# Sliding-window attention with a highway layer: gates of the first tiles a step later, other orders of loads, completions and the sinks' work, and a fused last tile

## The chip, the cores and the metric

The kernel runs on one core of a Trainium2 chip. The metric is the device time of one execution in microseconds; three runs of the kernel before have a median of 116.3 us (115.77 to 116.56). A profile of one further execution gives what every engine did and when; times inside it are counted from the start of its span.

## The reference

Attention over 4 batches, 8 heads, 768 positions and 64 values a head, in which a query sees the 4 first positions (the sinks) and the 128 positions up to its own. Its output, with the heads side by side, is the input x (3072 x 512) of a highway layer.

```python
scores = scale * np.matmul(q, k.transpose(0, 1, 3, 2))
keep = is_sink | in_window              # pos < 4, or 0 <= q_pos - k_pos < 128
scores = np.where(keep, scores, -1000000000.0)
a = softmax(scores)
x = (a @ v), heads side by side         # (3072, 512)
H = np.maximum(x @ w_h, 0.0)
T = 1.0 / (1.0 + np.exp(-(x @ w_t + b_t)))
out = T * H + (1.0 - T) * x
```

## The kernel before, in words

The 3072 rows are 24 tiles of 128 (N = 24, six to a batch, NC = 6). A loop of 26 steps, written out by hand (L471 to L544), is a pipeline: step n computes the scores of tile n, the attention output of tile n - 1 (`n1`), the gate and hidden products of tile n - 2 (`nb`), and completes an earlier tile. Every engine takes its instructions in the order in which the program has them; `_keep_traced_order` (L24) fixes that. So does each DMA queue: SP's, POOL's and, at the start, ACT's.

What a tile goes through, with the engine and the line:

- `scores` (L265, TensorE): a mask by matmul (L272) and q times k (L279) into `ps_s`, of which there is one; `expo` (L323, ACT) reads it into `E`.
- `starts` (L305, TensorE): the bias of the gate into `ps_z` (L311) and the sinks' part of the values into `ps_av` (L317).
- `values` (L330, TensorE, L338 and L341): `E` times `v`, which `cast_v` (L141) has cast from fp32, on VectorE for tiles 0 to 4 and on POOL from tile 5 on (`LATE`).
- `norm` (L346, VectorE): reciprocal of the sum (L349) and the product `X` (L351).
- `x_transpose` (L359, TensorE, L362) and `x_copy` (L365, ACT, L367): `XT`.
- `gate` (L369, TensorE, L371) into `ps_z`, `tanh` (L376, ACT, L378) into `TH`. The logistic function is 0.5 tanh(z / 2) + 0.5; the outer half is `gate_value` (L380), on VectorE, on POOL for the tiles in `POOL_GATES` (L73), and on ACT for the last two.
- `hidden` (L387, TensorE, L390) into `ps_h`, `diff` (L400, VectorE, L403): relu(hidden) - X into `DD`.
- `complete` (L423): `gate_value`, `gated` (L407, VectorE, L408: `DD` times `TH`), `finish` (L411, L414: plus `X`, on POOL, for tile 22 on VectorE) and the store by SP (L416).

The sinks of a batch need keys masked by head (`sink_keys`, L251), values masked by head (`sink_values`, L260, on POOL), the products of all queries with them (`sink_scores`, L286, L293) and an exponential (`sink_expo`, L299, L301). In step 2 of a batch they are made for tiles 2 to 5 (`sinks_at`, L452); for batch 0 it is done in two halves, in steps 2 and 4.

q and k come as fp32 and are cast to fp16 by loads on POOL's queue (`load_part`, L105; `load_rows` takes four of them), except the first two thirds of q of batch 0, which SP and ACT load as fp32. `transpose_qk` (L118, VectorE, L125) puts them where the scores read them; `units` (L429) says in which step which part is transposed, `loads` (L441) in which step which part is loaded. Batches 0 and 1 come in thirds, 2 and 3 in halves. V comes on SP's queue (`load_v`, L129), the two weights on POOL's (L194, L196). `completed` (L448) says which tiles a step completes: tile n - 6 in steps 6 to 12, 7 and 8 in step 13, n - 5 in steps 14 to 20, then two each in steps 21, 22 and 23 and tile 22 in step 24. `idle` (L418) issues matmuls on zeros, 18 before the loop, 5 in step 0, 3 in step 1. Tile 23 is completed behind the loop (L546 to L555).

Of the kernel before, what the change touches and what calls it, by code (L numbers as in the profile page):

```python
# [11 lines left out]
FP32 = mybir.dt.float32  # L12
# [25 lines left out]
def kernel(  # L38
# [33 lines left out]
    LATE = 5  # L72
    POOL_GATES = range(12, 16)  # L73

# [97 lines left out]
    def load_sinks(b, gs=range(G)):  # L172
        for g in gs:
# [5 lines left out]
              allow_small_or_imprecise_dtypes=True)  # L179
    load_rows(0, 0, 1)  # L180
    for g in range(G):
        pool.iota(vmask[32 * g:32 * g + 32, :], pattern=[[-NSINK, H]], base=0,
                  channel_multiplier=1, allow_small_or_imprecise_dtypes=True)
# [7 lines left out]
    pool.dma_start(out=brow[0:P:32, :], in_=moe_b_t.unsqueeze(0).to_broadcast([G, DM]))  # L191
    load_rows(0, 1, 1)
    load_rows(0, 2, 0)
# [46 lines left out]
    def sink_masks():  # L240
        dve.memset(skmask, 0.0)
        for g in range(G):
            for hg in range(HG):
                h = hg * G + g
                dve.memset(skmask[32 * g:32 * g + 32, hg, h:h + 1], 1.0)
# [134 lines left out]
    def gate_value(n):  # L380
        if n >= N - 2:
            act.activation(out=TH[n], in_=TH[n], func=AF.Copy, scale=0.5, bias=0.5)
        else:
            (pool if n in POOL_GATES else dve).tensor_scalar(  # L384
                out=TH[n], in0=TH[n], scalar1=0.5, scalar2=0.5, op0=ALU.mult, op1=ALU.add)
# [37 lines left out]
    def complete(m):  # L423
        gate_value(m)
        gated(m)
        finish(m, eng=dve if m == N - 2 else pool)


    units = {}  # L429
    for b in range(1, B):  # L430
        if b == 1:
            for n, i, which in zip((5, 5, 6, 7, 8, 9), (0, 0, 1, 1, 2, 2), (0, 1) * 3):
                units.setdefault(n, []).append((b, i, which))
        else:
# [11 lines left out]
    for n in range(8, N):  # L446
        v_at[n] = (n + 4,)
    completed = {n: (n - 6,) for n in range(6, 13)}  # L448
    completed[13] = (7, 8)
    completed.update({n: (n - 5,) for n in range(14, 21)})  # L450
    completed.update({21: (16, 17), 22: (18, 19), 23: (20, 21), 24: (22,)})
    sinks_at = {2: (0, (2, 3)), 4: (0, (4, 5))}  # L452
    for b in range(1, B):
        sinks_at[b * NC + 2] = (b, (2, 3, 4, 5))
# [3 lines left out]
    act.copy(out=nat[0][0][:, 0, 1], in_=first[0][:, 1])  # L458
    sink_masks()
    ones_columns()  # L460
# [3 lines left out]
    dve.tensor_copy(out=nat[0][1][:, 0], in_=first[1])  # L464
    transpose_qk(0, 1, 0)
    transpose_qk(0, 1, 1)
    sink_keys(0, dve)
    cast_v(0, dve)

    idle(18)  # L470
    for n in range(N + 2):  # L471

        nb, n1 = n - 2, n - 1
        if n < N:
# [5 lines left out]
            if n % NC == 3 and n // NC + 1 < B:  # L480
                load_sinks(n // NC + 1)
        if 4 <= n <= 6:
            hidden(n - 4 if n < 6 else 3)
        if n == 0:
            idle(5)
        starts(n1 if 0 <= n1 < N else None, nb if nb >= 0 else None)
        if 0 <= n1 < N:
            values(n1)
        if LATE <= n < N:
            cast_v(n, pool)  # L490
# [4 lines left out]
        for b, i, g, which in loads.get(n, ()):  # L495
            load_part(b, i, g, which)

        if 4 <= n <= 6:
            diff(n - 4 if n < 6 else 3)
        if n == 3:  # L500
            transpose_qk(0, 2, 1)
        turn = list(units.get(n, ()))
        if n == 5:
            transpose_qk(*turn.pop(0))
        if 0 <= n1 < N:
            norm(n1)
        if 0 < n < LATE:
            cast_v(n, dve)
# [4 lines left out]

        if nb >= 0:
            gate(nb)
            tanh(nb)
        if n == 5:
# [12 lines left out]
        if 6 <= n <= N:  # L530
            hidden(nb, range(KC // 2, KC))
        done = completed.get(n, ())
        for m in done[:-1]:
# [57 lines left out]
```

## Time and profile before

| | |
|---|---|
| median of three runs | 116.3 us (115.77 to 116.56) |
| the profiled execution | 114.55 us |
| its span | 112.8 us |
| TensorE clock granted, mean | 0.996 |
| TensorE matmul busy | 98.4 us (87%), 1414 instructions |
| VectorE busy | 87.5 us (78%), 184 instructions |
| ScalarE (ACT) busy | 76.6 us (68%), 95 instructions |
| GpSimd (POOL) busy | 87.2 us (77%), 141 instructions |
| moved by DMA | 20.81 MB, mean 185 GB/s |

A row of the timeline has the start, the time from the start of the first to the end of the last of the instructions that it merges, the engine and line, the operation, what is written from what, shapes, the count, and in brackets how long the engine had stood idle before it and what ended that. PE is TensorE, DVE is VectorE. Slices of the span show the busy share in tenths. A matmul's time in a row includes its way through the array, so that a row of TensorE rarely shows a short wait.

### The profile page before, as it was taken

How to read it: one execution, taken by the hardware profiler on the slowest of the kernel's cores; microseconds unless marked ns; L12 is line 12 of the kernel's file. 1: busy time of each engine (PE TensorE's matmuls, PEld its weight loads, DVE VectorE, ACT ScalarE, POOL GpSimd, SP SyncE). 2: the span in 40 equal slices, each digit the busy share in tenths (PEclk: the TensorE clock that was granted, in tenths of full speed). 3: DMA queues.
4: the chain of work that ended last, by engine and by line, in shares of the span. 5: the costliest groups of instructions: out<-in, count | busy, mean ns of one | idle time of the engine just before them, and what ended most of it. 6: DMA issues, size and time to landing. Idle time of an engine off the chain costs nothing.

```text
span 112.8 us, 3577 instructions
## 1 busy us (share of the span) xinstructions
PE 98.4 (87%) x1414; PEld 51.5 (46%) x1414; DVE 87.5 (78%) x184; ACT 76.6 (68%) x95; POOL 87.2 (77%) x141
## 2 busy tenths in 40 slices
PE   5986389899989998999999979999999999977900
PEld 2322246345435454655455535644555566523500
DVE  6796587535677986889998998699777979999660
ACT  4476639985557786788587868687678987842520
POOL 6899997249599499997899999999758965866100
PEclk9999999999999999999999999999999999999998
DMA  3999999999999749989998999899994503324222
GB/s 97 222 234 214 210 201 224 192 204 242 212 241 150 112 139 233 256 193 237 203 207 205 224 239 261 166 209 210 242 259 131 162 6 136 143 99 176 103 111 75
DMA packets 36704, 20.81 MB, mean 185 GB/s; under 512 B 27340, under 2 KB 33232, under 8 KB 36688
## 3 DMA queue, kind: packets, MB, share of 16 engines
q1 hardware_dynamic: 29680, 13.50, 46.6%
q0 software_dynamic: 6848, 6.82, 38.6%
q10 hardware_dynamic: 160, 0.26, 0.8%
q8 instruction: 11, 0.18, 0.7%
q14 instruction: 5, 0.04, 0.1%
HBM read 21.11 MB, written 6.29 MB: 243 GB/s over the span
## 4 chain that ended last, share of the span: by engine, by line
PE 39%; DVE 22%; POOL 14%; DMA 14%; issue 7%; DVEq 1%; POOLq 0%
POOL nat L109 11%; PE ps_h L390 9%; DMA wh<-in_moe_w_h_dram 9%; PE ps_z L371 8%; DVE tr L125 7%; PE ps_s L279 5%; DMA nat<-in_k_dram 5%; DVE DD L403 4%; DVE TH L384 4%; PE ps_av L341 4%; PE ps_av L338 3%; PE ps_s L272 3%; DVE DD L408 2%; PE ps_av L362 2%; DVE X L351 2%
## 5 line engine op out<-in xcount | busy, mean ns | idle before, releaser
L327 ACT ACTIVATE E<-ps_s,ebias 128x2048 f16<-128x2048 f32 (+1 forms) x24 | 43.8, 1825 | 12.6 <-PE ps_s L279 12.6
L414 POOL TENSOR_TENSOR O<-DD,X 128x512 f32<-128x512 f16 x22 | 25.4, 1156 | 10.1 <-DVE DD L408 4.2
L390 PE MATMUL ps_h<-wh,XT 128*128 128x512 f16 (+1 forms) x96 | 27.4, 375 | 0.2 <-DMA wh<-in_moe_w_h_dram 0.2
L125 DVE STREAM_TRANSPOSE tr<-nat 128x384 f32<-128x384 f32 (+1 forms) x28 | 25.7, 957 | 2.3 <-DMA nat<-in_k_dram 1.9
L109 POOL DMA_DIRECT2D nat<-in_k_dram x40 | 21.9, 554 | 5.5 <-DMA wh<-in_moe_w_h_dram 3.7
L371 PE MATMUL ps_z<-wt,XT 128*128 128x512 f16 x96 | 24.6, 379 | 0.0
L403 DVE SCALAR_TENSOR_TENSOR DD<-ps_h,X 128x512 f16<-128x512 f32 (+1 forms) x24 | 16.2, 673 | 8.2 <-PE ps_h L390 8.1
L367 ACT COPY XT<-ps_av 128x512 f16<-128x512 f16 x24 | 14.1, 586 | 7.8 <-PE ps_av L362 5.0
L378 ACT ACTIVATE TH<-ps_z 128x512 f16<-128x512 f32 x24 | 14.2, 592 | 7.4 <-PE ps_z L371 7.4
L109 POOL DMA_DIRECT2D nat<-in_q_dram x32 | 17.8, 562 | 0.8 <-DMA wt<-in_moe_w_t_dram 0.7
L351 DVE TENSOR_TENSOR X<-ps_av,rec 128x512 f16<-128x512 f32 x24 | 16.6, 692 | 1.0 <-DVE rec L349 0.2
L341 PE MATMUL ps_av<-v,E 128*128 128x65 f16 x192 | 14.1, 194 | 1.9 <-DVE v L142 1.8
L279 PE MATMUL ps_s<-tr 32*128 32x256 f16 (+1 forms) x384 | 14.5, 262 | 1.0 <-DVE tr L125 0.8
L341 PEld LDWEIGHTS <-E 128*128 128x128 f16 x192 | 11.8, 98 | 3.0 <-issue 3.0
L338 PE MATMUL ps_av<-v,E 128*128 128x65 f16 x160 | 12.7, 195 | 0.0
L408 DVE TENSOR_TENSOR DD<-DD,TH 128x512 f16<-128x512 f16 x24 | 11.9, 495 | 0.8
L338 PEld LDWEIGHTS <-E 128*128 128x128 f16 x160 | 10.2, 97 | 4.9 <-issue 4.9
L362 PE MATMUL ps_av<-ident,X 128*128 128x128 f16 x96 | 9.4, 221 | 3.2 <-DVE X L351 3.0
L142 POOL CAST v<-V 128x512 f16<-128x512 f32 x19 | 12.0, 633 | 0.0
L390 PEld LDWEIGHTS <-XT 128*128 128x128 f16 x100 | 8.7, 98 | 6.9 <-issue 0.7
L362 PEld LDWEIGHTS <-X 128*128 128x128 f16 x96 | 5.7, 97 | 12.2 <-DVE X L351 12.2
L371 PEld LDWEIGHTS <-XT 128*128 128x128 f16 x96 | 7.8, 98 | 6.0 <-ACT XT L367 0.3
(62 smaller groups left out, 100.9 us busy)
## 6 DMA issues: line engine op xcount, KB each, us to landing
V<-in_v_dram SPq DMA_DIRECT2D x24, 256.0 KB, 5.2
out_dram<-O SPq DMA_DIRECT2D x23, 256.0 KB, 2.8
nat<-in_k_dram POOLq DMA_DIRECT2D x24, 64.0 KB, 4.5
nat<-in_q_dram POOLq DMA_DIRECT2D x16, 96.0 KB, 4.2
nat<-in_k_dram POOLq DMA_DIRECT2D x16, 96.0 KB, 4.5
nat<-in_q_dram POOLq DMA_DIRECT2D x16, 64.0 KB, 4.9
first<-in_q_dram SPq DMA_DIRECT2D x6, 128.0 KB, 3.7
wt<-in_moe_w_t_dram POOLq DMA_DIRECT2D x1, 512.0 KB, 6.7
```

The source lines that it names most:

```text
L109: engine.dma_start(out=into[32 * g:32 * g + 32].rearrange("p hg m d -> p hg (m d)"), in_=(q, k)[which][b, :, t0:t0 + nt, :].rearrange("(hg ...
L125: dve.transpose(out=dst, in_=src)
L279: last = pe.matmul(ps_s[:, g, hg, 0:nq * P], lhsT=tr[b][rows, 1, hg, c * P:(c + 1) * P, e], rhs=tr[b][rows, 0, hg, c * P:(c + nq) * P, e], ...
L327: act.activation(out=E[n][:, :, :, 0:nq * P], in_=ps_s[:, :, :, 0:nq * P], func=AF.Exp, bias=ebias, scale=SCALE)
L338: pe.matmul(slot, lhsT=E[n - 1][:, g, hg, P:2 * P], rhs=v_of(n - 1)[:, h, :], start=first, stop=False, skip_group_check=True)
L341: pe.matmul(slot, lhsT=E[n][:, g, hg, 0:P], rhs=v_of(n)[:, h, :], start=first, stop=True, skip_group_check=True)
L351: dve.tensor_tensor(out=X[n], in0=av[:, :, :, 0:D], in1=rec.unsqueeze(3).to_broadcast([P, HG, G, D]), op=ALU.mult)
L362: pe.transpose(xt[:, kc // 2, (kc % 2) * P:(kc % 2 + 1) * P], x[:, kc * P:(kc + 1) * P], ident)
L371: pe.matmul(ps_z, lhsT=XT[n][:, kc * P:(kc + 1) * P], rhs=wt[:, kc, :], start=False, stop=(kc == KC - 1), skip_group_check=True)
L390: pe.matmul(into, lhsT=XT[n][:, kc * P:(kc + 1) * P], rhs=wh[:, kc, cols], start=(kc == 0), stop=(kc == KC - 1), skip_group_check=True)
L403: dve.scalar_tensor_tensor(out=DD[n][:, cols], in0=ps_h[:, cols] if h is None else h, scalar=0.0, in1=flat(X[n], cols), op0=ALU.max, op1=A ...
L414: eng.tensor_tensor(out=O[n][:, cols], in0=DD[n][:, cols], in1=flat(X[n], cols), op=ALU.add)
```

## The change

The gates of the first tiles go a step later: gate 0 to step 3, 1 to step 4, 2 and 3 to step 5, by the new function `layer_gate`, ahead of the values in steps 3 to 5. Hidden products 0 and 1 and their differences come behind the values and the norm in steps 4 and 5. In the preamble V of tile 0 is cast ahead of the transpose of k's second third, whose four loads are issued directly behind the first third's; the masks of the sinks' values are made later. Batch 0's sinks are done in step 2 at once. Two transposes of batch 1 come a step earlier. Tiles are completed in other steps, from step 5 on. The sinks' keys and values of the later batches are made at an earlier place on POOL, the values a step ahead of the keys. `gate_value` goes to POOL for tiles 14 to 21 and to ACT for tile 22 alone. For tile 23 the sum of tanh and 1 is fused with the product, and the half with the last sum, in two column halves, whose stores go out on two queues. There are 7 and 4 matmuls on zeros in steps 0 and 1.

```diff
-    POOL_GATES = range(12, 16)
+    POOL_GATES = range(14, 22)
...
     load_rows(0, 0, 1)
+    load_rows(0, 1, 1)
     for g in range(G):
         pool.iota(vmask[32 * g:32 * g + 32, :], pattern=[[-NSINK, H]], base=0,
...
     pool.dma_start(out=brow[0:P:32, :], in_=moe_b_t.unsqueeze(0).to_broadcast([G, DM]))
-    load_rows(0, 1, 1)
     load_rows(0, 2, 0)
...
     def gate_value(n):
-        if n >= N - 2:
+        if n == N - 2:
             act.activation(out=TH[n], in_=TH[n], func=AF.Copy, scale=0.5, bias=0.5)
...
+    def layer_gate(m):
+        starts(None, m)
+        gate(m)
+        tanh(m)
...
-            for n, i, which in zip((5, 5, 6, 7, 8, 9), (0, 0, 1, 1, 2, 2), (0, 1) * 3):
+            for n, i, which in zip((5, 5, 6, 7, 7, 8), (0, 0, 1, 1, 2, 2), (0, 1) * 3):
...
-    completed = {n: (n - 6,) for n in range(6, 13)}
-    completed[13] = (7, 8)
-    completed.update({n: (n - 5,) for n in range(14, 21)})
-    completed.update({21: (16, 17), 22: (18, 19), 23: (20, 21), 24: (22,)})
-    sinks_at = {2: (0, (2, 3)), 4: (0, (4, 5))}
-    for b in range(1, B):
+    completed = {5: (0,), 6: (1,), 8: (2, 3), 9: (4, 5), 15: (11, 12), 21: (18, 19)}
+    for n in range(10, 15):
+        completed[n] = (n - 4,)
+    for n in range(16, 21):
+        completed[n] = (n - 3,)
+    for n in range(22, N + 1):
+        completed[n] = (n - 2,)
+    sinks_at = {}
+    for b in range(B):
         sinks_at[b * NC + 2] = (b, (2, 3, 4, 5))
...
-    sink_masks()
+    dve.memset(skmask, 0.0)
+    for g in range(G):
+        for hg in range(HG):
+            h = hg * G + g
+            dve.memset(skmask[32 * g:32 * g + 32, hg, h:h + 1], 1.0)
     ones_columns()
...
     transpose_qk(0, 1, 0)
+    cast_v(0, dve)
+    sink_keys(0, dve)
+    sink_masks()
     transpose_qk(0, 1, 1)
-    sink_keys(0, dve)
-    cast_v(0, dve)
...
-        if 4 <= n <= 6:
-            hidden(n - 4 if n < 6 else 3)
+        if n == 6:
+            hidden(3)
         if n == 0:
-            idle(5)
-        starts(n1 if 0 <= n1 < N else None, nb if nb >= 0 else None)
+            idle(7)
+        if 3 <= n <= 5:
+            layer_gate(n - 3)
+        starts(n1 if 0 <= n1 < N else None, nb if n > 5 else None)
         if 0 <= n1 < N:
             values(n1)
+        if 4 <= n <= 5:
+            hidden(n - 4)
...
+        if NC <= n < N and n % NC == 0:
+            sink_values(n // NC)
+        if NC <= n < N and n % NC == 1:
+            sink_keys(n // NC)
+
+        turn, done = list(units.get(n, ())), list(completed.get(n, ()))
+        if n == 5:
+            transpose_qk(*turn.pop(0))
+        if n in (5, 6):
+            complete(done.pop(0))
+        if n == 6:
+            diff(3)
         if n == 3:
             transpose_qk(0, 2, 1)
...
         if 0 <= n1 < N:
             norm(n1)
+        if 4 <= n <= 5:
+            diff(n - 4)
...
-        if nb >= 0:
+        if n == 5:
+            layer_gate(nb)
+        if n > 5:
             gate(nb)
             tanh(nb)
-        if n == 5:
-            hidden(2)
         if n == 1:
-            idle(3)
+            idle(4)
...
+        if n == 5:
+            hidden(2)
         if 6 <= n <= N:
             hidden(nb, range(KC // 2, KC))
...
-        if n < N and n >= NC and n % NC == 0:
-            sink_keys(n // NC)
-        if n < N and n > NC and n % NC == 1:
-            sink_values(n // NC)
...
-    gate_value(last)
-    diff(last, left)
-    diff(last, right, h_right)
-    gated(last)
-    finish(last, left, dve)
-    finish(last, right, dve)
+    O[last] = work.tile([P, DM], FP32, tag="O", name="O")
+    for cols, h in ((left, None), (right, h_right)):
+        diff(last, cols, h)
+        dve.scalar_tensor_tensor(out=DD[last][:, cols], in0=TH[last][:, cols], scalar=1.0,
+                                 in1=DD[last][:, cols], op0=ALU.add, op1=ALU.mult)
+    for cols, engine in ((left, sp), (right, act)):
+        dve.scalar_tensor_tensor(out=O[last][:, cols], in0=DD[last][:, cols], scalar=0.5,
+                                 in1=flat(X[last], cols), op0=ALU.mult, op1=ALU.add)
+        engine.dma_start(out=out[last * P:, cols], in_=O[last][:, cols])
```

More of the change, by code (lines that the diff above doesn't have):

```diff
@@ L240, in sink_masks @@
     def sink_masks():
[L241 to L245, printed above, removed]
         dve.tensor_scalar(out=below, in0=vmask, scalar1=float(NSINK - 1), scalar2=None,
@@ L496 @@
             load_part(b, i, g, which)
-        if 4 <= n <= 6:
-            diff(n - 4 if n < 6 else 3)
+        if NC <= n < N and n % NC == 0:
[9 more added lines that the diff above has]
+            diff(3)
         if n == 3:
             transpose_qk(0, 2, 1)
-        turn = list(units.get(n, ()))
-        if n == 5:
-            transpose_qk(*turn.pop(0))
         if 0 <= n1 < N:
             norm(n1)
+        if 4 <= n <= 5:
+            diff(n - 4)
         if 0 < n < LATE:
@@ L512 @@
             transpose_qk(*unit)
-        if nb >= 0:
+        if n == 5:
+            layer_gate(nb)
+        if n > 5:
             gate(nb)
             tanh(nb)
-        if n == 5:
-            hidden(2)
         if n == 1:
-            idle(3)
+            idle(4)
         if 6 <= n <= N:
@@ L529 @@
                 sink_expo(*sinks_at[n])
+        if n == 5:
+            hidden(2)
         if 6 <= n <= N:
             hidden(nb, range(KC // 2, KC))
-        done = completed.get(n, ())
         for m in done[:-1]:
```

## The prediction, on record before the changed kernel was run

> **What bounds the kernel now.** "Step n" is the loop's n; it begins with the scores of tile n (L272 rows). I read the page first, for shares and slices.
>
> ```profile
> span 112.8 us, 3577 instructions
> PE 98.4 (87%) x1414; PEld 51.5 (46%) x1414; DVE 87.5 (78%) x184; ACT 76.6 (68%) x95; POOL 87.2 (77%) x141
> ...
> PE   5986389899989998999999979999999999977900
> ...
> DMA  3999999999999749989998999899994503324222
> ```
>
> TensorE is the bound in the middle, not in the first 32 us nor after 97 us; the DMA engines are full for the first 36 us. So I read the waits and the timeline of the three stretches. First the start: V of tile 0 is cast behind a transpose that waits for k's second third, and TensorE stands 1.8 us.
>
> ```profile
> 12.29 1.10 DVE L125 STREAM_TRANSPOSE tr<-nat 128x512 f32<-128x512 f32 x1 [1.90 <-DMA nat<-in_k_dram]
> ...
> 13.47 0.41 DVE L142 CAST v<-V 128x512 f16<-128x512 f32 x1
> ...
> 13.93 0.42 PE L341 MATMUL ps_av<-v,E 128*128 128x65 f16 x8 [1.82 <-DVE v L142]
> ...
> 24.09 0.53 POOL L109 DMA_DIRECT2D nat<-in_k_dram  x1 [3.67 <-DMA wh<-in_moe_w_h_dram]
> ```
>
> The last line is POOL's: its 27th load waits for the 19th (wh) to land; the 22nd waited for the 14th (wt), the 35th for the 27th. POOL thus reaches step 5's cast only at 32.21. From there to 78 it idles 3.1 us in all (1.49, 1.19, 0.19, 0.24 before four rows of L414): in steps 5 to 16 it is nearly as full as TensorE.
>
> Then the middle: three steps are long.
>
> ```profile
> 44.12 0.42 PE L293 MATMUL ps_av<-tr,sk 128*32 128x64 f16 x30 [0.46 <-DVE tr L125]
> ...
> 66.23 0.40 PE L362 MATMUL ps_av<-ident,X 128*128 128x128 f16 x4 [0.59 <-DVE X L351]
> ...
> 67.51 1.05 POOL L261 TENSOR_TENSOR vs<-vs,vmask 128x520 f16<-128x520 f32 x1
> ...
> 68.52 0.68 POOL L142 CAST v<-V 128x512 f16<-128x512 f32 x1
> ```
>
> Step 8 waits for a transpose of batch 1's q, step 14 for X (two completions in step 13 kept DVE), step 15 for V's cast behind two results and the sinks' values. They take 4.68, 4.75 and 4.29 us; step 20, of 8's and 14's kind, takes 4.00 and steps 9 and 21, of 15's kind, 3.53. So 0.68 + 0.75 + 0.75 = 2.2 us.
>
> Last the end: DVE carries two completions a step, slowly, and TensorE waits for X.
>
> ```profile
> 98.92 0.43 DVE L408 TENSOR_TENSOR DD<-DD,TH 128x512 f16<-128x512 f16 x1
> ...
> 100.25 0.40 PE L362 MATMUL ps_av<-ident,X 128*128 128x128 f16 x4 [0.67 <-DVE X L351]
> ...
> 102.05 0.91 DVE L384 TENSOR_SCALAR TH<-TH 128x512 f16<-128x512 f16 x1
> ...
> 103.00 0.43 DVE L408 TENSOR_TENSOR DD<-DD,TH 128x512 f16<-128x512 f16 x1
> ...
> 104.32 0.40 PE L362 MATMUL ps_av<-ident,X 128*128 128x128 f16 x4 [0.70 <-DVE X L351]
> ```
>
> **The change part by part.** The profiled execution took 114.55 us (span 112.8 and 1.75 around it); the three runs have a median of 116.3. I work in its span and take the difference off the median.
>
> *Start.* The four issues of k's second third (2.1 us on POOL) go ahead of four iotas, the identity and the bias row (1.9 us), which come 2.1 us later and are first used after 12 us: nothing. Loads 10 and up keep place and number, so POOL's waits stay; only the 0.26 us before load 15 may go. SP's queue keeps its order. With the DMA engines full, k's 256 KB (1.2 us at some 214 GB/s) can hold back what else lands then: q's second third (about 8.5) and V 0 (about 10.0), by 0 to 1.2. I take 0.5 to 1. On DVE two mask operations (0.35) move back, so the first transposes start 0.3 earlier; V 0's cast ends near 11.5 instead of 13.9; the transpose of k runs 12.2 to 13.3, as before, now behind cast, sinks' keys (0.31) and masks. X of tile 0 then ends at 14.3 (15.32), and scores 2 begin at 14.7 (15.71). Without a gate in step 2, scores 3 begin at 18.0 (19.14); the sinks' scores are 32 matmuls there instead of 16 (0.43 against 0.42 us by the rows, their bank rows side by side) and none in step 4 (0.41 less; one ACT exponential of 0.36 less). Step 3 takes gate 0 (1.0) before values 2, so scores 4 come at 22.1 (22.75); V 3 lands about 23.0, and its cast, due at 24.1, holds. Scores 5: 26.3 (27.57). Step 5 then owes a gate more than before: scores 0.65, gate 1.05, values 0.75, hidden 0.85, gate 1.0, X's transpose 0.35, hidden 0.9: scores 6 at 31.9, without the 0.3 us wait for q and k (transposed by 31.6). They end at 32.8 against 33.25: **0.4 us** gained, bounds +0.5 (V 0 late by 1.2) and -1.3 (what step 5's start shows). The three added warm-up matmuls (0.21 each) lie under an exponential of 1.97.
>
> *Middle.* Transposes 1.1 us each: q's last third goes from step 8 to 7, k's from 9 to 8. Step 8's wait goes (sinks' keys, now early in step 7, end at 43.0; needed at 43.3). Completions: tiles 0 and 1 in steps 5 and 6, none in 7, two in 8, 9, 15 and 21. Each costs DVE 0.28 + 0.43 and POOL a result of 1.11. Doubles now meet at most one transpose (step 8: DVE 4.1 us in a step of 4.0, a lag of 0.1 to 0.5, before TensorE needs X). Step 13 has a single one, so 14's wait goes; sinks' values come ahead of the completion in step 12, so 15's goes.
>
> What is late next is POOL: in-order, it issues two more results (2.2 us) by step 16. From 32.21, with cast 0.55, load 0.545, result 1.11, sinks' values 1.05, keys 0.5 and idle 0.6 where a product is not ready, cast 10 ends at 52.4 and cast 16 at 74.6. TensorE needs cast 10 at 52.1 and cast 16 at 74.3, where it would be by the removed waits. So step 16's values start at 74.6 against 76.1, and from step 18 on the kernel is **1.6 us** early: start and middle together, not 0.4 + 2.2. Bounds: 0 (POOL keeps its 3.1 us of idle) and -2.6.
>
> *End.* DVE's gates 16 to 21 (0.46 to 0.92 each) go to POOL, where four rows show 0.62, and steps 22 and 23 complete one tile instead of two. POOL has 2.3 us a step here (cast, gate, result). DVE's products now wait for POOL's gates, with the next norm behind them: tile 20's gate follows its tanh at step 22 + 3.7 and ends at + 4.3; DVE finishes diff 20 at + 4.7, so it does not wait. In step 21 the second gate sits behind a result, which delays the next norm 0.45 us and TensorE 0.1. From scores 23, X's transpose of tile 22 comes at + 2.55 (before + 3.32, 100.25 - 96.93) and, through ACT's copy, values, gate and half a hidden product, tile 23's at + 5.65 (before + 7.39). **1.65 us** gained with the 0.1 off; bounds -0.8 (only tile 22's part) and -1.75.
>
> *Tail.* The last gate value on ACT (0.63) goes; DVE runs six operations of 256 columns. Independent ones start 0.34 apart (107.11, 107.45), dependent ones 0.49. From 107.11: 107.60, 107.93, 108.42, 108.75, 109.08, end 109.5 against 109.24; the second half's store no longer queues behind the first on SP (0.37), but that was under DVE. **+0.25 us**. The price of the fused form on two fp16 operands in SBUF is not in the trace. Rows on both sides: 0.29 (L217, 128 columns, two fp32 operands in SBUF) and 0.69 (L414 on DVE, 512 columns); I take 0.42, what 256 columns cost at L403 and L414. Bounds -0.1 and +1.3 (four at 0.69: 1.1 more).
>
> The Trainium skill's page "Vector Engine (DVE) Microarchitecture Reference", section "Points that are easy to get wrong", says that this fused form runs at half rate with two non-bf16 operands in SBUF. By it the sum would lie near the upper bound, an estimate. L217's 0.292 us for 128 columns, near the 0.277 of L207, which reads one operand, does not show that.
>
> Sum: -1.6 - 1.65 + 0.25 = -3.0. Span 109.8, profiled 111.55, median **113.3 us**.
>
> **Rivals.** *POOL late, end kept.* POOL idles as it did and pays the two results: cast 16 at 74.6 + 2.5 = 77.1, and start and middle give nothing or less. 0 - 1.65 + 0.25: 114.9. For it: POOL's 93% between 32 and 78. Against: its old idle was waiting for completions, which now come earlier.
> *End lost.* Products of tiles 18 to 21 wait for POOL's gates, and norm behind them, by 0.8 us in steps 22 and 23: 116.3 - 1.6 + 0.25 = 114.95. Against: 2.3 us of POOL work in steps of 3.5.
> *Tail slow.* The four fused operations with both operands in SBUF cost 0.69 instead of 0.42: 1.1 more, 114.4. Against: L217. The skill's rule above would bring it about.
> *Slower.* One mechanism, POOL's queue falling behind, reaches both ends: cast 16 at 77.7 is 1.6 us later than now's 76.1, and still late in step 21, DVE, which now waits for its gates, keeps its old pace: +1.6 + 0 + 0.25, 118.2. It decides against the change from about 3 us of lag on my walk. Against: steps 17 to 20 leave POOL about 1 us each to catch up.
> *Better.* POOL starts step 5 earlier or casts faster, so start and middle give their 2.6: 112.3.
>
> **How the numbers follow.** As summed 0.55 (112.4 to 114.2 by its own bounds), better 0.10, tail slow 0.05, POOL late 0.14, end lost 0.08, slower 0.08. A measurement here tells about 1% from nothing: 115.1 and 117.5. Faster: 0.55 + 0.10 + 0.05 and six tenths of the 0.22 near 114.9, 0.83; same 0.09; slower 0.08. The range 111.8 to 115.4 takes in all but the slower case and tails.
>
> **What would show it.** Right: scores 6 near 31.9; no 1.8 us wait for V 0; step 8 about 4.0 us, 14 about 4.0, 15 about 3.5; cast 16 ending at 74 to 75; no wait for X at tiles 22 and 23; the last stretch from scores 23 to X 23 near 5.7 us; fused operations of 0.42 us. Wrong: TensorE's values waiting for POOL's casts by more than 0.5 us, DVE's products waiting on POOL's gates in steps 21 to 23, wh landing later than 23.8, or fused operations near 0.69.

## The result, and the profile after

The changed kernel takes **117.49 us** (median of 20 runs, 115.91 to 119.42), the kernel before on the same chips 115.62 (20 runs): a ratio of 1.014, 95% interval 1.0097 to 1.0183. It is slower by 1.4%, where 113.3 us and 2.6% faster were forecast. (The medians are of all runs; the ratio compares the faster runs of both, without those in a slower state that some executions of either kernel show.) The profiled execution took 118.03 us (span 116.2), 3.4 us of span over that of before; a fall of TensorE's clock in it, which is not in all executions, is dealt with below.

The page of the changed kernel, busy time first and then slices of 2.9 us:

```profile
span 116.2 us, 3582 instructions
...
PE 100.6 (87%) x1417; PEld 51.8 (45%) x1417; DVE 88.5 (76%) x181; ACT 75.7 (65%) x93; POOL 88.8 (76%) x145
...
PE   5998667599999999996999999968999999799910
...
PEclk9999999968999999999999999999999999999999
```

Every engine has about the share that it had. The clock's dip stands in slices 9 and 10, and TensorE has holes in slices 19, 27 and 35 that before does not have. These are the starts of tiles' scores (step n begins there) and the lengths of the steps that differ, read from TensorE's timeline:

| us | before | after | x3 | y2 | y3 |
|---|---|---|---|---|---|
| scores 6 begin | 31.94 | 35.35 | 33.00 | 33.94 | 35.09 |
| step 5 | 4.37 | 5.78 | 5.78 | 5.79 | 5.77 |
| steps 8, 14, 15 | 4.68, 4.75, 4.29 | 4.01, 4.00, 3.53 | 4.01, 3.99, 3.54 | 4.24, 4.16, 3.65 | 4.02, 4.00, 3.53 |
| steps 9, 10 | 3.53, 3.60 | 3.83, 4.90 | 3.97, 4.89 | 3.83, 3.64 | 3.74, 3.54 |
| steps 16, 17 | 3.54, 3.45 | 5.33, 3.47 | 5.32, 3.47 | 3.53, 4.10 | 3.90, 3.46 |
| step 22 | 3.56 | 4.39 | 4.38 | 3.65 | 3.64 |
| scores 23 begin | 96.93 | 102.30 | 99.85 | 99.70 | 98.31 |
| from there to X 23 | 7.39 | 5.66 | 5.66 | 5.63 | 5.66 |

(x3, y2 and y3 are experiments, below.) So the start lost 3.4 us; the middle gained the 2.2 us of steps 8, 14 and 15 and lost 4.2 in steps 9, 10, 16 and 22; the end gained 1.7.

The start, from the timelines of DVE, TensorE and POOL of the changed kernel:

```profile
10.66 0.85 DVE L471 CAST nat<-first 128x1024 f16<-128x1024 f32 x1 [2.22 <-DMA first<-in_q_dram]
...
12.70 0.64 PE L274 MATMUL ps_s<-tr 32*128 32x256 f16 x16 [1.09 <-DVE tr L125]
...
14.13 1.06 POOL L109 DMA_DIRECT2D nat<-in_k_dram  x2 [1.82 <-DMA brow<-in_moe_b_t_dram]
...
21.39 1.10 DVE L125 STREAM_TRANSPOSE tr<-nat 128x512 f32<-128x512 f32 x1 [2.25 <-DMA nat<-in_k_dram]
...
23.30 0.40 PE L357 MATMUL ps_av<-ident,X 128*128 128x128 f16 x4 [1.44 <-DVE X L346]
```

V's cast no longer holds TensorE. But q's second third now lands at 10.6, and the scores of tile 1 wait 1.09 us for its transpose, so that scores 2 come at 15.69 (15.71 before) and nothing is won. Then the bias row's load stops POOL's issues for 1.82 us, k's last third is transposed at 21.39, and X of tile 2, queued behind that on DVE, makes TensorE wait.

The middle: DVE in step 9, with its two completions, then TensorE's waits for X in steps 10, 16 and 22:

```profile
50.47 0.62 DVE L379 TENSOR_SCALAR TH<-TH 128x512 f16<-128x512 f16 x1
51.12 0.71 DVE L403 TENSOR_TENSOR DD<-DD,TH 128x512 f16<-128x512 f16 x1
...
52.36 0.91 DVE L379 TENSOR_SCALAR TH<-TH 128x512 f16<-128x512 f16 x1
53.31 1.30 DVE L403 TENSOR_TENSOR DD<-DD,TH 128x512 f16<-128x512 f16 x1
```

```profile
55.50 0.40 PE L357 MATMUL ps_av<-ident,X 128*128 128x128 f16 x4 [1.18 <-DVE X L346]
...
79.04 0.40 PE L357 MATMUL ps_av<-ident,X 128*128 128x128 f16 x4 [1.62 <-DVE X L346]
...
101.53 0.40 PE L357 MATMUL ps_av<-ident,X 128*128 128x128 f16 x4 [0.68 <-DVE X L346]
```

Gate values and products that take 0.28 and 0.43 elsewhere take 0.62 to 1.30 here: 3.54 us for four operations instead of 1.42. POOL's rows of the same stretch say why:

```profile
49.80 1.14 POOL L409 TENSOR_TENSOR O<-DD,X 128x512 f32<-128x512 f16 x1 [0.70 <-DVE DD L403]
50.89 0.67 POOL L142 CAST v<-V 128x512 f16<-128x512 f32 x1
51.51 1.62 POOL L109 DMA_DIRECT2D nat<-in_q_dram  x3
53.14 1.17 POOL L409 TENSOR_TENSOR O<-DD,X 128x512 f32<-128x512 f16 x1
```

Add start and duration on both sides. POOL's operations end at 50.94, 51.56, 53.13 and 54.31; DVE's end at 51.09, 51.83, 53.27 and 54.61. Each of DVE's ends 0.14 to 0.30 us after one of POOL's: it began while POOL was at work and got on only when POOL was done.

### The profile page after: what moved, and what is told of

It is laid out like the page before. It is cut to its first block, busy times and chain, and to the rows that moved or that the text cites. A ratio compares the mean times of both kernels' runs of the same rounds, so it can differ in the third digit from the quotient of the medians.

```text
span 116.2 us, 3582 instructions
## 1 busy us (share of the span) xinstructions
PE 100.6 (87%) x1417; PEld 51.8 (45%) x1417; DVE 88.5 (76%) x181; ACT 75.7 (65%) x93; POOL 88.8 (76%) x145
## 4 chain that ended last, share of the span: by engine, by line
DMA 27%; POOL 20%; DVE 19%; PE 17%; issue 13%; ACT 1%; DVEq 1%; POOLq 0%
DMA nat<-in_q_dram 10%; DMA wh<-in_moe_w_h_dram 8%; POOL nat L109 8%; DMA brow<-in_moe_b_t_dram 5%; DVE tr L125 5%; PE ps_h L385 4%; PE ps_z L366 4%; POOL v L142 4%; POOL O L409 4%; DMA nat<-in_k_dram 3%; POOL TH L379 3%; DVE DD L398 3%; DVE TH L379 2%; DVE X L346 2%; PE ps_s L274 2%
## 5 line engine op out<-in xcount | busy, mean ns | idle before, releaser
L366 PE MATMUL ps_z<-wt,XT 128*128 128x512 f16 x96 | 25.5, 389 | 0.0
L398 DVE SCALAR_TENSOR_TENSOR DD<-ps_h,X 128x512 f16<-128x512 f32 (+1 forms) x24 | 16.1, 671 | 4.2 <-PE ps_h L385 4.2
L109 POOL DMA_DIRECT2D nat<-in_q_dram x32 | 17.2, 546 | 0.9 <-DMA nat<-in_q_dram 0.6
L403 DVE TENSOR_TENSOR DD<-DD,TH 128x512 f16<-128x512 f16 x23 | 12.9, 560 | 3.6 <-POOL TH L379 2.8
```

The source lines that it names most:

```text
L109: engine.dma_start(out=into[32 * g:32 * g + 32].rearrange("p hg m d -> p hg (m d)"), in_=(q, k)[which][b, :, t0:t0 + nt, :].rearrange("(hg ...
L366: pe.matmul(ps_z, lhsT=XT[n][:, kc * P:(kc + 1) * P], rhs=wt[:, kc, :], start=False, stop=(kc == KC - 1), skip_group_check=True)
L398: dve.scalar_tensor_tensor(out=DD[n][:, cols], in0=ps_h[:, cols] if h is None else h, scalar=0.0, in1=flat(X[n], cols), op0=ALU.max, op1=A ...
```

## The experiments

Theory A: the doubled completions cost what they do because DVE's gates and products are held up by POOL's work beside them; the start is lost by the loads' order and by the later gates. Theory B: DVE simply has too much to do in those steps. Each kernel's ratio is to the kernel before, run on the same chip. Line numbers shift by a few in some kernels.

**x1: the loads as before.** The changed kernel, with

```diff
-    load_rows(0, 1, 1)          # behind the first third
+    load_rows(0, 1, 1)          # behind the bias row
```

> The changed kernel, but with the four loads of k's second third back behind the bias row's load; all else as changed. Theory A (the start is lost on POOL's queue and in the full DMA engines because these four loads went ahead): scores 6 begin near 32 us of the span instead of 35.4, no wait of 1.8 us of POOL for the bias row, q's second third is there near 8.5 us instead of 10.6, and the time falls by 1.5 to 3 us, to 114.5 to 116. Rival B (the start is lost because gates a step later leave TensorE idle and its granted clock halved between 24 and 27 us): the clock still drops, scores 6 stay later than 34 and the time stays above 116.5. Rival C (all is lost in the middle): no change, 117.5.

118.47 us (116.28 to 120.09), of which no ratio is to be had, and a profile with the clock at 0.50 from 17.9 to 21.3 us. q's second third is there at 8.6 again and the bias row stops nothing, but what that is worth can't be read from it; x5 asks again, with the completions of before as well.

**x2: the completions as before.**

```diff
-    completed = {5: (0,), 6: (1,), 8: (2, 3), 9: (4, 5), 15: (11, 12), 21: (18, 19)}
...
+    completed = {n: (n - 6,) for n in range(6, 13)}
...
-    POOL_GATES = range(14, 22)
+    POOL_GATES = range(12, 16)
```

> The changed kernel, but with the list of completions and the tiles whose gate value is POOL's as before. Theory A (steps 10, 16 and 22 are long since two completions in the step ahead run on VectorE beside POOL's results and take 2 us each): steps 10 and 16 fall from 4.9 and 5.3 us to about 3.6, steps 14 and 15 go back to 4.7 and 4.3, and the stretch from scores 23 to the transpose of X 23 goes back from 5.7 to 7.4 us; the sum is about 0, 117 to 118. Rival (completions do not matter, the doubled steps are long for another reason, such as V's loads): steps 10 and 16 stay above 4.5 us and the time rises to about 119.

116.84 us, ratio 1.0121 (1.0058 to 1.0184). Steps 10 and 16 are 3.54 each, step 14 5.46 (the wait of 15 moved into it), and from scores 23 to X 23 it takes 7.40. So the long steps and the gain at the end both come from the completions and the gate values moved with them. The kernel is still slower than before, with the changed front and without the gain at the end.

**x3: the bias row's load ahead of k's second third.**

```diff
+    pool.dma_start(out=brow[0:P:32, :], in_=moe_b_t.unsqueeze(0).to_broadcast([G, DM]))
     load_rows(0, 1, 1)
...
-    pool.dma_start(out=brow[0:P:32, :], in_=moe_b_t.unsqueeze(0).to_broadcast([G, DM]))
```

> The changed kernel, but with the bias row's load issued ahead of k's second third, which still goes ahead of the iotas. Theory A1 (POOL's 17th load waits for its 9th, which is now the bias row's, landing late): POOL's wait of 1.8 us goes, wh is issued near 13.7 us instead of 15.2, k's last third lands 1 to 2 us earlier, and the time falls by 0.7 to 1.7 us. Rival A2 (the four loads displace q's second third and V 0 in the full DMA engines, whatever the queue): q's second third still lands near 10.6, scores 1 stay at 12.7 and the time falls by less than 0.5 us.

116.49 us, ratio 1.011 (1.0036 to 1.0183), which the times can't tell from the changed kernel's 1.014. POOL's wait for the bias row is gone. Scores 7 stand 0.65 us behind before, in x2 2.10 behind, both without a fall of the clock. But 1.05 of these 1.45 us are there at scores 2 (14.65 against 15.70), ahead of any use of the load that waited: q's second third landed 0.96 us earlier (9.77 against 10.73), between what A1 and A2 say. And k's last third is transposed at 20.59 here, at 20.94 in x5, which has no such wait either, against 21.39. So what POOL's wait itself costs is not shown. Steps 10, 16 and 22 are as long as ever.

**x4: the kernel before with the new completions and tail.**

```diff
-    completed = {n: (n - 6,) for n in range(6, 13)}
...
+    completed = {5: (0,), 6: (1,), 8: (2, 3), 9: (4, 5), 15: (11, 12), 21: (18, 19)}
...
-    POOL_GATES = range(12, 16)
+    POOL_GATES = range(14, 22)
```

> The kernel before with only the list of completions, the tiles whose gate value is POOL's, and the last tile's fused end of the changed one. If the parts add up, by what the traces show: the end gains 1.7 us and the tail 0.2, steps 10, 16 and 22 lose about 1.3, 1.8 and 0.8, steps 14 and 15 gain 0.7 each: 0 to +0.5 us against the kernel before, that is same. Rival (without the lost start the doubles find the room that the prediction gave them): 1.5 to 3 us faster than before.

117.56 us, ratio 1.0177 (1.0111 to 1.0242), against an expectation of near zero: steps 10 and 16 take 5.15 and 5.46 here, step 9 4.05, and step 8, whose transposes stay, gains nothing. The new completions and gate values, with a tail that by itself costs nothing that can be told (w2), make the kernel slower.

**x5: x2 with the loads as before as well**, so that the early loop and the tail are new.

> The changed kernel with the loads in the order of before and with the completions and POOL's gates of before, so that only the early loop (gates a step later, V first, sinks' scores at once, units, sinks' values) and the tail are new. Theory A (the lost start came from the order of the loads, the lost middle from the doubled completions): scores 2 near 14.7, scores 6 at 32 to 33 in a stretch without a fall of the clock, steps 8, 14 and 15 as in the run with only the completions undone; the time 114.3 to 115.3 against 115.6 of before. Rival B (the early loop itself costs: step 5 owes a gate more and takes 5.78 us instead of 4.37, whatever the loads do): scores 6 at 33.5 or later, and the time 116 to 117.

115.95 us, ratio 1.0024 (0.9975 to 1.0072). Between the two ranges expected. Step 5 takes 5.78, step 8 is 0.27 shorter, and what step 15 gains step 14 loses; the early loop as a whole costs nothing that can be told. Against x2 (1.0121), which differs in the place of k's second third alone, the loads' order is worth some 1%, though the two intervals meet; scores 7 stand at 38.33 against 39.13.

**x6: the kernel before with V first alone.**

```diff
-    transpose_qk(0, 1, 1)
-    sink_keys(0, dve)
     cast_v(0, dve)
+    sink_keys(0, dve)
+    transpose_qk(0, 1, 1)
```

> The kernel before with one edit: V of tile 0 is cast, and the sinks' keys made, ahead of the transpose of k's second third. Theory A: scores 2 at 14.7 (before 15.71), since V 0 lands near 10.0 as before; the gain is worn down by what lands later (V 3 near 23.0, k's last third near 19.1) to 0 to 0.5 us at scores 6, and the time is 115.1 to 115.6. Rival B (a microsecond won at step 2 lasts to the end): scores 6 at 31.0 and 114.5. A third way, that POOL's queue sets step 5 and later: scores 6 unchanged at 31.9, and the time that of before.

115.36 us, ratio 0.9939 (0.9888 to 0.999). Scores 2 come at 14.47, 1.2 us earlier, and TensorE then stands before gate 0, whose weights land when they land:

```profile
19.05 1.02 PE L371 MATMUL ps_z<-wt,XT 128*128 128x512 f16 x4 [2.94 <-DMA wt<-in_moe_w_t_dram]
```

In x8, whose front is the same, this wait is 0.71 and scores 6 come at 31.87 (before 31.94; in x6 itself 33.06): a microsecond won at step 2 is a later wait for the loads.

**x7: x3 with the gates of 4, 5, 11 and 12 on ACT**, where the completion issues them.

```diff
-        if n == N - 2:
+        if n in (4, 5, 11, 12, N - 2):
             act.activation(out=TH[n], in_=TH[n], func=AF.Copy, scale=0.5, bias=0.5)
```

> The changed kernel with the bias row's load ahead of k's second third, and the gate values of tiles 4, 5, 11 and 12 (the doubles of steps 9 and 15) on ACT instead of DVE: 0.63 us each there by the row of tile 22. Theory A (DVE's gates and products are slow in those steps since POOL's results run beside them): the gates go, the two products still take 0.7 to 1.3 us beside POOL's results, steps 10 and 16 come down by half of their excess, from 4.9 to 4.2 and from 5.3 to 4.5, and the time is 115.2 to 115.8 (116.5 with the gates on DVE). Rival B (DVE has simply two operations too many): the products fall back to 0.43, steps 10 and 16 take 3.6, and the time is 114.0 to 114.8. Rival C (ACT, with two more operations in a step, becomes late with its exponentials): steps 9 and 15 take 4.5 and nothing is gained.

117.22 us, ratio 1.0075 (1.003 to 1.0121): a miss for A and B both, though for a reason that the rows show. ACT is in order, and the gates stand behind the step's exponential, tanh and copy:

```profile
52.27 0.42 DVE L403 TENSOR_TENSOR DD<-DD,TH 128x512 f16<-128x512 f16 x1 [1.68 <-ACT TH L377]
...
53.21 1.35 DVE L403 TENSOR_TENSOR DD<-DD,TH 128x512 f16<-128x512 f16 x1
```

The second product, begun 0.11 after a result of POOL's (53.10 to 54.27), still takes 1.35; the first, beside DMA issues of POOL's only, 0.42.

**x8: a candidate** on before: V first, sinks' values ahead, transposes in 5 to 8, the second result of each double on DVE.

```diff
+    completed.update({9: (3, 4), 15: (10, 11), 21: (17, 18), 22: (19, 20), 23: (21,), 24: (22,)})
...
-        finish(m, eng=dve if m == N - 2 else pool)
+        finish(m, eng=dve if m in (4, 11, 18, 20, N - 2) else pool)
```

> The kernel before, its loads, gates and tail as they were, with V first as in the other kernel of this set, the transposes of batch 1 in steps 5 to 8, the sinks' values and keys ahead of the completions, and completions five steps behind from step 9, four from 15, three at 21 and two from 22: where two meet, both gates come first (those of 4 and 11 on ACT, 16 to 21 on POOL) and the second result is DVE's. Theory A: step 8 at 4.0, 14 at 4.0 and 15 at 3.6 (before 4.68, 4.75, 4.29) without a long step in return, and from scores 23 to X of tile 23 5.7 us (before 7.4): 112.0 to 113.0 us. Rival B (DVE carries the second results no better than it carried the gates): steps 10, 16 and 22 long by 0.7 each, 113.5 to 114.5.

118.48 us, ratio 1.0263 (1.0162 to 1.0365), the worst of all. The result on DVE, 0.69 where POOL is idle, took 1.47 at 51.46 beside one on POOL from 51.12 to 52.37, and TensorE waited 1.13 for X in step 10. Both theories had it faster than before. More such work on DVE is the wrong way.

**y3: x3 without the results** of tiles 2 to 5, 11, 12, 18 and 19.

```diff
-        finish(m, eng=dve if m == N - 2 else pool)
+        if m not in (2, 3, 4, 5, 11, 12, 18, 19):
+            finish(m, eng=dve if m == N - 2 else pool)
```

> The changed kernel with the bias row's load ahead of k's second third, and without the results of tiles 2, 3, 4, 5, 11, 12, 18 and 19: their sums on POOL and their stores are left out, so those rows of the output are missing; DVE has all its gates and products as in the changed kernel. Theory A: in steps 9, 15 and 21 DVE's gates and products come back towards 0.28 and 0.43 us where no result runs beside them, and steps 10, 16 and 22 take 3.6 to 3.9 (4.9, 5.3 and 4.4 with the results); the time is 113.5 to 114.5 against 116.5. Rival B (two completions are too much for DVE, whatever POOL does): gates and products as slow as before or the steps still above 4.5, and 115.5 or more.

114.34 us, ratio 0.9853 (0.9762 to 0.9944; x3 1.011). DVE's four operations of step 9 in y3:

```profile
50.10 0.28 DVE L379 TENSOR_SCALAR TH<-TH 128x512 f16<-128x512 f16 x1
50.42 0.42 DVE L403 TENSOR_TENSOR DD<-DD,TH 128x512 f16<-128x512 f16 x1
...
51.72 0.28 DVE L379 TENSOR_SCALAR TH<-TH 128x512 f16<-128x512 f16 x1
52.04 0.43 DVE L403 TENSOR_TENSOR DD<-DD,TH 128x512 f16<-128x512 f16 x1
```

The same four operations, 1.41 us instead of 3.54, and steps 10, 16 and 22 at 3.54, 3.90 and 3.64. DVE had room for two completions; what it did not have was the time in which POOL works. A holds, B falls.

**y2: x3 with six gates on ACT right behind their tanh**, steps before they are due.

```diff
     def tanh(n):
         TH[n] = work.tile([P, DM], FP16, tag="TH", name="TH", bufs=8)
         act.activation(out=TH[n], in_=ps_z, func=AF.Tanh, scale=0.5)
+        if n in (4, 5, 11, 12, 18, 19):
+            act.activation(out=TH[n], in_=TH[n], func=AF.Copy, scale=0.5, bias=0.5)
```

> The changed kernel with the bias row's load ahead of k's second third, and the gate values of 4, 5, 11, 12, 18 and 19 on ACT right behind their tanh, steps before their products are due. Theory A: the products beside POOL's results still take 0.7 to 1.35 us, but DVE is free of the gates (0.6 to 0.9 each), so that steps 10, 16 and 22 come from 4.9, 5.3 and 4.4 to 3.6 to 4.1, and the time from 116.5 to 114.3 to 115.2. Rival B (DVE's room is used up by the two products alone, or POOL's queue is what is late): steps 10 and 16 stay above 4.5 and the time at 116 or more.

114.82 us, ratio **0.984** (0.9728 to 0.9952). The products of step 9 are as slow as A says (0.76 and 1.26), but without the gates DVE is in time: steps 10, 16 and 22 take 3.64, 3.53 and 3.65. ACT's gate of 0.63 lies mostly where its copy waited for TensorE; steps 8 and 14 are 0.2 longer than in x3. Six operations moved turn 1.011 into 0.984.

**y1: a candidate** on before, with V first, its loads and its early gates, and six gates on ACT.

```diff
+    ACT_GATES = (3, 4, 10, 11, 17, 18)
...
+    completed = {6: (0,), 8: (1, 2), 9: (3, 4), 15: (10, 11), 21: (17, 18),
+                 22: (19,), 23: (20,), 24: (21, 22)}
```

> Before's kernel with V first, the transposes of batch 1 in steps 5 to 8, the sinks' values and keys ahead of the completions, completions doubled in steps 8, 9, 15, 21 and 24 with none in 7, and the gate values of tiles 3, 4, 10, 11, 17 and 18 on ACT right behind their tanh (14 to 16 and 19 to 21 on POOL). Theory A (what made the doubled steps long is DVE's slow gates and products beside POOL, and without the gates DVE has room): steps 7, 8, 9, 10, 14, 15, 16 at 3.3, 4.0, 3.6, 3.8, 4.0, 3.6, 3.8 us, from scores 23 to X of tile 23 5.7, and 112.5 to 113.5 us. Rival C (ACT becomes late by its gates, 0.6 us in a step in which it has about 0.8 idle ahead of its copy): steps 5, 6, 12, 13, 19 and 20 each longer by 0.3 to 0.6, and 114.5 to 116.

114.63 us, ratio 0.9863 (0.9769 to 0.9957), against 112.5 to 113.5 us expected. Step 7 takes 4.60, by one gate value left on DVE:

```profile
37.45 1.77 DVE L389 TENSOR_SCALAR TH<-TH 128x512 f16<-128x512 f16 x1
```

It starts while POOL issues three DMAs (36.40 to 37.98), and POOL's sinks' values follow at once (37.99 to 39.06); it ends at 39.22, 0.16 after those.

**z1, z2, z3: the front.** z1 is the front of before with V first and the completions of after, gates 0, 1, 4, 5, 11, 12, 18 and 19 on ACT; z2 is y2 with the loads as before; z3 is z2 with

```diff
-        if n == 1:
-            idle(4)
+        if n in (1, 2, 3):
+            idle(4 if n == 1 else 6)
```

> The front, the loads and the tail of before with V first, and behind step 6 the changed kernel's completions, units, sinks' values and POOL's gates; the gate values of tiles 0, 1, 4, 5, 11, 12, 18 and 19 on ACT right behind their tanh. Theory A (gates a step later only put work off from a stretch in which TensorE waits for loads into step 5, where it doesn't): scores 6 at 31.7 to 32.0, step 5 at 4.4, step 7 at 3.3 to 3.6, steps 10, 16 and 22 at 3.6 to 3.9, scores 23 at 95.5 to 96.5, and 112.3 to 113.5 us. Rival (the later gates are no loss in themselves, only the loads' order was): no better than the next kernel of this set.

> The changed kernel with the loads in the order of before and the gate values of 4, 5, 11, 12, 18 and 19 on ACT right behind their tanh: the early gates are still a step later, with V first. Theory A: step 5 at 5.8 as in every kernel with the later gates, scores 6 at 33.0 to 34.0, 1.2 to 2 us behind the kernel with before's front, and 113.8 to 114.8 us. Rival (the later gates are no loss): scores 6 at 32.3 or earlier, and 113.0.

> The kernel before this one of the set with six more idle matmuls of TensorE in each of steps 2 and 3, ahead of X's transpose, where it waits 1.1 and 1.5 us. Theory W (the granted clock falls to 0.5 near 24 us in a part of the executions, because TensorE stood idle from 20.7 to 22): the clock stays 1.0 through 20 to 28 us, and the time is 0.5 to 1.0 us under that of the kernel without them, 113.2 to 114.0. Rival (the fall doesn't come from those waits): the same time within 0.3 us, or later by the part of the 1.3 us of matmuls that isn't under a wait.

114.72, 115.32 and 114.43 us; ratios 0.9892 (0.9848 to 0.9935), 0.99 (0.9837 to 0.9963) and 0.9916 (0.9879 to 0.9954). The times tell none of them from another, and each is above its theory's range. The profiles do show the later gates' price where the clock stayed up; TensorE's rows of scores 5 and 6, first in y1 (gates as before), then in w1 (gates a step later):

```profile
27.28 0.29 PE L273 MATMUL ps_s<-mq,mk 32*128 32x256 bf16 x4
...
31.64 0.40 PE L273 MATMUL ps_s<-mq,mk 32*128 32x256 bf16 x8
```

```profile
27.35 0.29 PE L268 MATMUL ps_s<-mq,mk 32*128 32x256 bf16 x4
...
33.13 0.40 PE L268 MATMUL ps_s<-mq,mk 32*128 32x256 bf16 x8
```

4.36 against 5.78 us for step 5. By scores 10 nothing is left of it: from scores 5 it is 22.05 us in y1 and 21.70 in z1 (before's gates), 21.95 in w1 and 21.85 in z3 (later gates). Step 7 of y1 and step 9 of z1 (4.70) are long, each with a gate value on DVE that POOL held up (1.77 and 1.73).

z2's profile has the fall of the clock at its longest. These are stretches of 2 us with TensorE's busy time, the other engines', the granted clock, and DMA; z2 first, then z3:

```profile
16.00:18.00 2.00, 0.66 (x16) 0.48 (x14) 1.95 (x5) 1.93 (x1) 1.37 (x3) 0.70 1.23 213
18.00:20.00 2.00, 1.89 (x52) 1.41 (x56) 0.46 (x2) 0.69 (x2) 1.82 (x4) 0.50 1.22 218
...
30.00:32.00 2.00, 2.00 (x20) 1.19 (x21) 0.35 (x2) 0.60 (x1) 2.00 (x5) 0.50 1.05 179
```

```profile
16.00:18.00 2.00, 1.42 (x21) 0.94 (x20) 1.95 (x4) 1.89 (x1) 1.81 (x4) 1.00 1.23 220
18.00:20.00 2.00, 2.00 (x64) 1.14 (x61) 0.64 (x2) 0.81 (x3) 1.67 (x4) 1.00 1.23 222
```

The clock is 0.50 for some 15 us in z2 after a stretch in which TensorE was busy for a third, and scores 6 begin at 39.49; in z3 it stays. But z3's ratio is no better than z1's or z2's, and the kernel before had a mean clock of 0.976 (median of 23 runs), lower than z3's 0.990. The fall explains single executions, not the 1.4%.

**w1 and w3: a result behind a cast.** In y2 step 17 takes 4.10, with TensorE waiting for a cast. w1 puts tile 13's result behind the cast of V 17, w3 tile 12's behind that of V 16.

```diff
         if LATE <= n < N:
             cast_v(n, pool)
+        if n == 16:
+            finish(12)
```

> The changed kernel with the bias row's load ahead of k's second third, the gate values of 4, 5, 11, 12, 18 and 19 on ACT right behind their tanh, and the result of tile 13 on POOL behind the cast of V 17 instead of ahead of it. Theory A (the last cost of the double in step 15 is that two results, 2.28 us, stand ahead of that cast, for which TensorE waits 0.59): step 17 at 3.5 instead of 4.1, no wait for that cast, and 0.984 of before less 0.005, about 113.3 us at a before of 115.7. Rival (POOL's lag only moves on, to the next cast): step 18 or 19 longer by what step 17 loses, and the ratio 0.984 to 0.99.

> As the run before, with the result that matters: tile 12's goes behind the cast of V 16, and tile 13's stays where it was. In the run before, the two results ahead of the cast for which TensorE waited in step 17 were those of tiles 11 and 12, and the cast V 16's. Theory A (the order on POOL): step 17 at 3.5, the wait of 0.59 gone, and some 0.6 us less than that kernel, a ratio near 0.98. Rival (POOL's lag only moves on): steps 18 to 20 longer by 0.3 to 0.6, and a ratio of 0.985 to 0.99 as before.

w1: 114.52 us, ratio 0.9874 (0.981 to 0.9939), step 17 unchanged: the cast that TensorE waits for is V 16's, behind the results of 11 and 12. It was the wrong one; TensorE's and POOL's rows of w1:

```profile
76.58 0.19 PE L337 MATMUL ps_av<-v,E 128*128 128x65 f16 x1 [0.59 <-POOL v L143]
```

```profile
73.69 2.29 POOL L414 TENSOR_TENSOR O<-DD,X 128x512 f32<-128x512 f16 x2
75.92 0.61 POOL L143 CAST v<-V 128x512 f16<-128x512 f32 x1
```

w3: 114.68 us, ratio 0.9888 (0.9844 to 0.9932). Step 17 falls to 3.69 and step 19 grows from 3.39 to 3.81: the rival was right, POOL's lag only moves on. With DVE freed, what POOL has to do seems to set these steps.

**w2: the kernel before with the new tail alone.**

```diff
-    gate_value(last)
-    diff(last, left)
-    diff(last, right, h_right)
-    gated(last)
...
+        dve.scalar_tensor_tensor(out=DD[last][:, cols], in0=TH[last][:, cols], scalar=1.0,
+                                 in1=DD[last][:, cols], op0=ALU.add, op1=ALU.mult)
```

> The kernel before with the changed tail alone: the fused operations with tanh + 1, without the last gate value on ACT, the second store on ACT's queue. The forecast's term: DVE's chain 0.25 us longer, bounds -0.1 and +1.3; from the profiles of the changed kernel 0.2 longer with the stores ending as before: a ratio of 0.998 to 1.004, from scores 23 to the end of the span 15.9 to 16.2 us (before 15.87). Rival (the second store, no longer behind the first, ends the span earlier): 0.2 to 0.5 us less than before.

115.79 us, ratio 1.0014 (0.9971 to 1.0057). DVE's last chain runs from 108.04 to 110.45, 2.41 us against 2.13 (107.11 to 109.24): 0.28 more. The fused operations:

```profile
108.56 0.43 DVE L553 SCALAR_TENSOR_TENSOR DD<-TH,DD 128x256 f16<-128x256 f16 x1
...
109.36 0.43 DVE L553 SCALAR_TENSOR_TENSOR DD<-TH,DD 128x256 f16<-128x256 f16 x1
```

## Why the prediction was wrong, point by point

- **"Each costs DVE 0.28 + 0.43 ... Doubles now meet at most one transpose."** This is the step that failed and turned the sign. Transposes were not what kept DVE. With POOL at work a pair in steps 9 and 15 cost 1.33 to 2.21 us instead of 0.71, and steps 9, 10 and 16 grew by 3.4 us in all. y3 and y2 show it from two sides: take away POOL's work or DVE's gates, and the steps are short. Both start from x3; with the loads as changed, the moved gates were not run, and x2 says that with that front the completions of before are slower than before too. The rows of before that the forecast itself quotes (0.91 and 0.92 for a gate value) already said that 0.28 is not the price beside POOL; they were read as a feature of the end.
- **"Loads 10 and up keep place and number, so POOL's waits stay."** Wrong. The bias row came into another place of POOL's loads, and the load eight places on waited 1.82 us for it. How much of the loads' price this is stays open (x3): the loads' order as a whole is worth 0.8 us at scores 7 by x5 and some 1% of the time.
- **"Scores 5: 26.3."** Undelivered: 27.2 to 27.4 in x3 and w1, which have neither the bias row's wait nor a fall of the clock; what holds them is not pinned down (TensorE waits 1.68 us for X of tile 2 in x3, behind the transpose of k's last third, and 1.30 in w1, where that transpose is long done). The bounds for the start were too narrow: k's second third was let ahead of q's at 0 to 1.2 us, and q's was late by 2.1 (10.6 against 8.5; 8.4 to 9.4 in the profiles with the loads as before). That ate what V's earlier cast won. It is the second step that failed.
- **"Step 5 then owes a gate more":** right, 5.78 us against 5.6 worked out. But it was offset against a start that did not come.
- **Middle, the waits removed:** right, 0.67, 0.75 and 0.76 us against 2.2 in sum. **What is late next** was named as POOL's casts; in the changed kernel TensorE waits for no cast of POOL's in steps 16 and 17. They were next in y2 and w1, once DVE was free: 0.59 us.
- **End:** right, 5.66 us against 5.65 from scores 23 to X 23. Its side cost was sized at 0.1 (step 21's second gate behind a result); DVE's product waited 1.26 us for that gate, which the forecast lists among its signs of being wrong, and step 22 grew by 0.83.
- **Tail:** right, +0.28 against +0.25, with 0.42 to 0.43 a fused operation. The Trainium skill's page "Vector Engine (DVE) Microarchitecture Reference" has, in the section that the forecast names, half the rate for two operands in SBUF that are not bf16. Here the form took 0.42 to 0.43 us with two fp16 operands in SBUF and 0.42 with one in PSUM, so the half rate is not seen; no run has bf16 operands to compare.
- **The rivals:** none held as a whole. Of "End lost" the wait for POOL's gates came true, with 0.83 us in step 22, but from scores 23 on the gain held. "Slower" came to the right side by the wrong mechanism, POOL's queue; the forecast had no rival in which POOL slows DVE rather than TensorE.

**What it adds up to**, in the profiled span: +3.4 at scores 6, -2.2 and +4.2 in the middle, -1.7 at the end: 3.7, with the span 3.4 longer. Of the 3.4, x2, which has the same front and no fall of the clock, shows 2.5 (34.45), and x3, with the bias row's load ahead, 1.1 (33.00); the 0.9 beyond x2 are most likely the fall, in which gate 1 took 1.89 us instead of 1.03. The medians differ by 1.9 only: before's profiled execution lies 1.1 us under its median, the changed kernel's 0.5 over.

A version that beats both kernels is y2: the change with the bias row's load in its old place and six gate values on ACT, 1.6% faster than before (0.5 to 2.7%, from few runs; w1 and w3, which add one moved result, are 1.1 to 1.3% faster). How far the early part in itself helps or harms stays open: the kernels that differ in it alone lie within each other's intervals.

## What to carry to other kernels

Price an operation of VectorE by a row in which GpSimd does what it will do beside it, not by its shortest row: here the difference is a factor of two to three, and it decided the sign. Work that can be done early on an engine with idle time just ahead of a wait (a gate value right behind its tanh) is cheap there, and dear if it is issued where it is due, behind that engine's next long operation. Before moving a load, count the places of its queue: a small load in a new place can hold the load that reuses its place.

## What the runs showed of the hardware

- GpSimd's computing holds up some operations of VectorE altogether: gate values, products and V's casts end 0.14 to 0.30 us after GpSimd's operation, whether they began 0.4 or 1.9 us before that. The normalisation and the differences, whose first input lies in PSUM, kept their 0.66 to 0.69 throughout. The Trainium skill's page "SBUF — State Buffer", section "Who interferes with whom", names one pair of ports that the two engines share, locked for a whole instruction, and says that an operation of VectorE with two inputs in SBUF contends with one of GpSimd that reads SBUF. The products agree with it; the gate value and V's cast, with one input, were held up as well. The longest such operation is a cast of V in x5, 2.23 us instead of 0.42 (from 14.19 to 16.42, beside GpSimd's sinks' values until 16.13).
- While GpSimd issues DMAs the gate value is held up too (0.91 us; 1.77 where sinks' values follow). Of products beside issues alone two took 0.42 and 0.43 (x7) and two 0.87 and 1.26 (y2), which stays unexplained.
- TensorE's clock falls to half in some executions after a stretch of low use, for 3 us or for 15, and not in others: in x6 TensorE stood idle from 16.1 to 19.05 us at a clock of 1.00 throughout. The Trainium skill's page "TensorE: Matmul & The Clock Gate", section "What's actually happening", has the clock follow the busy share of a window that runs freely, so that the same kernel varies from run to run. That some executions fall and others don't agrees with it; the window itself is in no trace.
